# Second copies of k and q by DMA within SBUF, and one block of p's high part on ScalarE

## The chip, the core and the metric

One core of one Trainium2 chip runs the whole program in a single launch. The metric is the device time of the launch in microseconds. Five engines work beside each other, each through its own list of instructions in order: PE (TensorE, matrix products), DVE (VectorE), ACT (ScalarE), POOL (GpSimd) and SP (SyncE, which here issues DMAs). They wait for each other by semaphores.

## The reference

Causal attention with a decay for 4 batches of 8 heads (sequence 576, head size 64), then two MLPs over the 2304 tokens, all in float32:

```python
scores = scale * np.matmul(q, k.transpose(0, 1, 3, 2))
decay = cum[:, :, :, None] - cum[:, :, None, :]        # cum: running sum of log f
scores = np.where(causal, -1000000000.0, scores + decay)
attn = np.exp(scores - max) ; attn = attn / (sum + 1e-09)
x = attn @ v
h = x @ w_in ; x = (max(h, 0) + alpha * min(h, 0)) @ w_out
out = ((x @ w_a) * (x @ w_b)) @ w_o
```

## The kernel before

**Stages.** The program runs attention head by head (32 heads, `u` from 0 to 31, two further rounds to drain). The first MLP runs in two parts: a first part (7 of its 16 blocks of columns) is woven into the attention stage and fills PE between the steps of the heads, as soon as the four batches' attention outputs are there one after the other; the rest, and the second MLP, follow by themselves. The attention stage ends at about 350 us of the span.

**One head.** `stack(n)` turns q and k of head n: PE transposes them into a PSUM bank (`tqk`, two halves of 288 columns), and from there they go to SBUF in the form that the products want. From head 10 on (`NATIVE = 10`) a float32 product is made of parts. k's high part goes to `u1` in partitions 64 to 127 (ACT, line 350) and k's remainder to `u2` (DVE, 353); q's high part goes to `t1` in partitions 0 to 63 (ACT, 352) and its remainder to `t1` in partitions 64 to 127 (DVE, 355). Two second copies complete the operands: `u1`'s high part again in partitions 0 to 63 (POOL, called in line 358 and recorded in line 238 by the helper `dup`), and q's high part again in `t2` (ACT, called in line 357, recorded in line 234). `products` then takes two matmuls for each block of scores: `t1` by `u1` over 128 partitions (line 372) and `t2` by `u2` over 68 (line 373; the last four of these partitions carry the decay). Heads 0 to 9 take a shorter way without second copies.

**Softmax and p.** `softmax_in` masks a block on DVE (385) and exponentiates it on ACT (386). `rinv` makes the reciprocals (DVE, 408 and 409). For a head from 10 on, `p_hi` writes the high half-precision part of each of the five blocks of p (ACT in line 438, or POOL in 440) and `p_lo` the remainder (DVE, 520). When the parts of a group of blocks are there, SP issues a DMA that transposes them (527), and `pv` multiplies by v two heads later. Blocks are numbered by their width: block 3 is 128 rows by 512 columns, block 2 is 128 by 384. An engine for each step stands in the table `eng`, over which `eng0` is laid for steps 0 to 9.

**What sets the order.** The lists `even` and `odd` say in which order the steps of a head are written; a scheduler with a model of times then interleaves them into one order for each engine, which the chip follows as it stands. Tiles named with `_0` or `_1` serve even and odd heads in turn. All DMAs are issued by SP. The scheduler gives the DMAs eight semaphores in turn, and a DMA waits until the one before it on its semaphore has landed.

```python
pe.matmul(o, t1[:, q0:q0 + 128], u1[:, a0:a1], start=start, stop=False)
pe.matmul(o, t2[0:68, q0:q0 + 128], u2[0:68, a0:a1], start=False, stop=stop)
```

Of the kernel before, what the change touches and what calls it, by code (L numbers as in the profile page):

```python
# [40 lines left out]
    odd="ri h3 h2 h0 R rr vs h1 M Q l2 T l3 s2 M h4 s3 l1 M M s1 l0 s0 p0 p1 V W po l4 M".split(),  # L41
    split=0,
    lag=2,
    eng={'U': 'pool', 'xl': 'pool', 'h2': 'act', 'h0': 'pool', 'h1': 'pool', 'nq': 'act', 'x': 'dve'},
    psm=3,
    first=10,
    rates=[0, 1, 1, 1, 0.8, 1.15, 1.15, 0.95],
# [2 lines left out]
    pre=1,  # L50
    we=0,
    es=10,
    eng0={'h3': 'pool', 'U': 'pool', 'h1': 'pool', 'e0': 'act', 'e2': 'act', 'e3': 'dve', 'e4': 'dve'},
    even0=['ri', 's3', 'T', 'p0', 'h2', 'h3', 's2', 'vs', 'h1', 's0', 'Q', 'M', 'M', 'M', 'M', 'l1', 'l2', 'h0', 's1', 'l0', 'l3', 'p1', 'V', 'po', 'W', 'M'],
    odd0=['ri', 'h3', 'h2', 'h0', 'R', 'h1', 'rr', 'M', 'Q', 'l2', 'T', 'l3', 'M', 's3', 'h4', 's2', 'l1', 'l0', 'M', 'M', 's1', 's0', 'p0', 'vs', 'p1', 'V', 'W', 'po', 'l4', 'M'],
)
# [3 lines left out]
NATIVE = _P.get("native", 0)  # L60
# [20 lines left out]
def f32(ap):  # L81
    return ap.bitcast(F32)
# [3 lines left out]
def decay_attention_then_two_mlps(ctx, tc, q, k, v, f, w_in, w_out, alpha, w_a, w_b, w_o, out):  # L86
    nc = tc.nc
    pe, dve, act, pool, sp = nc.tensor, nc.vector, nc.scalar, nc.gpsimd, nc.sync

    left, mid, right = ExitStack(), ExitStack(), ExitStack()  # L90
    def lpool(stack, name, bufs, side="left", **kw):
        return stack.enter_context(tc.tile_pool(name=name, bufs=bufs, side=side, reuse_waits="tile", **kw))
# [133 lines left out]
    def eng(key, default):  # L226
        d = _P["eng"]
        if ap_["u"] < _P.get("es", 0):
            d = dict(d, **_P.get("eng0", {}))
        return {"pool": pool, "act": act, "dve": dve}[d.get(key, default)]  # L230

    def dup(e, o, i):
        if e is act:
            act.copy(o, i)
        elif e is dve:
            dve.tensor_copy(o, i)
        else:
            pool.tensor_scalar(o, i, 1.0, 0.0, op0=ALU.mult, op1=ALU.add)
# [82 lines left out]
    def bank(nm):  # L321
        return ps["at"].tile([128, 512], F32, tag="at", name=nm)

    def stack(n):

        src = nat.pop(n)
        j = n % 2
        t1, t2, u1, u2, tu2 = TU[j]
        if n < NATIVE:
            t2, u2, tu2 = TUN[j]  # L330
        if n >= 2:
            sp.dma_start(tu2[64:68, :SP + S], cum_d[j][n // 2])
        for c in range(2):
            a0, a1 = c * HB, (c + 1) * HB
            pt = bank(f"tqk_{n}_{c}")[:, :HB]
            for t in range(TM):
                rows = src[:, c * TM + t].rearrange("p i d -> p (i d)")
                pe.transpose(pt[:, t::TM], rows, ap_["ident"][:TT, :TT])
            qt, kt = pt[0:64], pt[64:128]
            ks = slice(a0, a1)  # L340
            cuts = [(a0, a1, 0)]
            if c == 1 and j == 1:
                cuts = [(a0, ST, 0), (ST, a1, SR)]
            cuts = [(slice(x - a0, y - a0), slice(x + o, y + o)) for x, y, o in cuts]
            if n < NATIVE:
                dup(eng("nk", "act"), u2[0:64, ks], kt)
                for x, o in cuts:
                    dup(eng("nq", "act"), t2[0:64, o], qt[:, x])
                continue
            act.copy(u1[64:128, ks], kt)  # L350
            for x, o in cuts:
                act.copy(t1[0:64, o], qt[:, x])
            dve.tensor_tensor(u2[0:64, ks], kt, f32(u1)[64:128, ks], op=ALU.subtract)
            for x, o in cuts:
                dve.tensor_tensor(t1[64:128, o], qt[:, x], f32(t1)[0:64, o], op=ALU.subtract)
            for x, o in cuts:
                dup(eng("T2", "act"), t2[0:64, o], qt[:, x])
            dup(eng("U", "pool"), u1[0:64, ks], f32(u1)[64:128, ks])

    def s_view(n, i):  # L360
        if i == 4:
# [247 lines left out]
    def attention():  # L609

        cur = lambda u: 0 <= u < NI
        if LAG == 2:
            load_v(0)
        warm_up(_P.get("wu", [0, 0])[0], "a")
        stack(0)
        warm_up(_P.get("wu", [0, 0])[1], "b")
        load_qk(2)
        yield "W", -1
        for u in range(NI + LAG):
            ap_["u"] = u  # L620
            for op in order(u):
# [10 lines left out]
                elif a in "hl":  # L632
                    if cur(u - 1):
                        (p_hi if a == "h" else p_lo)(u - 1, int(i))
                elif op == "R":
                    if cur(u):
                        softmax_rest(scores_rest(u))
                elif op == "rr":
                    if cur(u):
                        rinv(ap_["smr"][:, 0:1], ap_["rir"][:, 0:1])  # L640
                elif a == "s":
                    if cur(u):
                        softmax_in(u, int(i), scores(u, int(i)))
                elif op == "T":
                    if cur(u + 1):
                        stack(u + 1)
                elif op == "Q":
                    if u and cur(u + 2):
                        load_qk(u + 2)
                elif op == "V":  # L650
                    if cur(u + 3 - LAG):
                        load_v(u + 3 - LAG)
                elif op == "vs":
                    if cur(u + 2 - LAG):
                        split_v(u + 2 - LAG)
                elif op in ("p0", "p1"):
                    if cur(u - LAG):
                        pv(u - LAG, int(i))
                elif op == "po":
                    if cur(u - LAG):  # L660
                        pv_out(u - LAG)
# [68 lines left out]
    if True:  # L730
# [192 lines left out]
        for ri, (p, t0, n) in enumerate(runs):  # L923
            f0, f1 = PASSES[p]
            xh, xl = cur
# [168 lines left out]
```

## Time and profile before

| what | value |
|---|---|
| time, median of 3 runs | 1062.86 us (1062.18 to 1063.13) |
| the profiled execution: time | 1065.95 us |
| the profiled execution: span of its instructions | 1064.1 us |
| PE busy over the span | 1022.4 us, 96% |
| DVE, ACT, POOL busy over the span | 713.4, 487.2, 497.3 us |
| mean granted TensorE clock | 0.997 of full speed |

The span runs from the first to the last instruction of the profiled execution; the rest of its time, 1.85 us, lies around it. Busy time says how long an engine had an instruction in hand; idle time before an instruction is put down to the event that came last. A time in the trace counts from the span's start.

### The profile page before, as it was taken

How to read it: one execution, taken by the hardware profiler on the slowest of the kernel's cores; microseconds unless marked ns; L12 is line 12 of the kernel's file. 1: busy time of each engine (PE TensorE's matmuls, PEld its weight loads, DVE VectorE, ACT ScalarE, POOL GpSimd, SP SyncE). 2: the span in 40 equal slices, each digit the busy share in tenths (PEclk: the TensorE clock that was granted, in tenths of full speed). 3: DMA queues.
4: the chain of work that ended last, by engine and by line, in shares of the span. 5: the costliest groups of instructions: out<-in, count | busy, mean ns of one | idle time of the engine just before them, and what ended most of it. 6: DMA issues, size and time to landing. Idle time of an engine off the chain costs nothing.

```text
span 1064.1 us, 18614 instructions
## 1 busy us (share of the span) xinstructions
PE 1022.4 (96%) x6447; PEld 958.6 (90%) x6447; DVE 713.4 (67%) x1518; ACT 487.2 (46%) x1200; POOL 497.3 (47%) x566
## 2 busy tenths in 40 slices
PE   4999989999999999999999998999999999999998
PEld 3777989989989999999999998899989999899997
DVE  6667988888888456444456558755986658964553
ACT  5777867778777554333343443322432113321110
POOL 4344567567676355333446766522443224531111
PEclk9999999999999999999999999999999999999999
DMA  5545577876877766656667996726328383453623
GB/s 113 135 121 165 141 138 138 202 146 133 180 164 122 210 222 199 224 191 199 186 230 258 340 365 249 304 94 237 103 94 317 113 310 111 137 206 139 247 89 109
DMA packets 221698, 196.27 MB, mean 184 GB/s; under 512 B 138980, under 2 KB 195812, under 8 KB 221604
## 3 DMA queue, kind: packets, MB, share of 16 engines
q1 hardware_dynamic: 221604, 195.08, 61.2%
q8 instruction: 51, 0.84, 0.3%
q14 instruction: 43, 0.35, 0.1%
HBM read 126.83 MB, written 50.17 MB: 166 GB/s over the span
## 4 chain that ended last, share of the span: by engine, by line
PE 52%; DVE 8%; DMA 3%; issue 3%; POOL 2%; ACT 1%; ACTq 0%; DVEq 0%; POOLq 0%; SPq 0%
PE p L674 7%; PE p L676 7%; PE p L675 7%; PE o L676 4%; PE o L674 4%; PE o L675 4%; PE ya L674 3%; PE ya L675 3%; PE ya L676 3%; PE hb L674 3%; PE hb L676 3%; PE hb L675 3%; DMA wr_in<-in_moe_w_in 2%; DMA yq_d<-yhl 1%; POOL yhl L881 1%
## 5 line engine op out<-in xcount | busy, mean ns | idle before, releaser
L674 PE MATMUL p<-yq,w_h 128*128 128x384 f32 x360 | 121.8, 338 | 2.2 <-DVE lu L1043 1.3
L676 PE MATMUL p<-yq,w_h 128*128 128x384 f32 x360 | 121.3, 337 | 0.0
L675 PE MATMUL p<-yq,w_h 128*128 128x384 f32 x360 | 121.2, 337 | 0.0
L1025 POOL TENSOR_TENSOR gg<-tc,gg 128x384 fp32r<-128x384 f32 x36 | 36.7, 1019 | 114.0 <-ACT gg L1024 96.8
L674 PE MATMUL o<-w_o,gg 128*128 128x512 f32 x216 | 84.7, 393 | 1.7 <-ACT gg L1024 1.7
L675 PE MATMUL o<-w_o,gg 128*128 128x512 f32 x216 | 84.8, 393 | 0.0
L671 POOL TENSOR_TENSOR gb<-lt,gb 128x384 fp32r<-128x384 f32 x54 | 55.5, 1028 | 60.4 <-ACT gb L670 60.3
L676 PE MATMUL o<-w_o,gg 128*128 128x512 f32 x216 | 83.2, 393 | 0.0
L1025 POOL TENSOR_TENSOR gg<-td,gg 128x384 fp32r<-128x384 f32 x36 | 38.1, 1059 | 89.5 <-ACT gg L1024 83.7
L386 ACT ACTIVATE s<-s,nm 128x512 f32<-128x512 f32 (+3 forms) x128 | 71.4, 559 | 10.1 <-DVE nm L385 9.3
L1024 ACT CAST gg<-tc 128x384 fp32r<-128x384 f32 x36 | 18.5, 514 | 124.7 <-DVE tc L1023 124.7
L674 PEld LDWEIGHTS p<-yq,w_h 128*128 128x128 f32 x360 | 67.6, 188 | 6.9 <-DVE lu L1043 1.7
L669 DVE SCALAR_TENSOR_TENSOR lt<-lu,nal,hb 128x384 f32<-128x384 f32 x54 | 33.0, 611 | 59.8 <-ACT lu L668 59.8
L675 PE MATMUL ya<-gb,w_out 128*128 128x384 f32 x216 | 72.7, 337 | 0.0
L676 PE MATMUL ya<-gb,w_out 128*128 128x384 f32 x216 | 72.5, 336 | 0.0
L674 PE MATMUL ya<-gb,w_out 128*128 128x384 f32 x216 | 71.0, 336 | 1.2 <-DVE yl L866 1.2
L675 PEld LDWEIGHTS p<-yq,w_h 128*128 128x128 f32 x360 | 67.6, 188 | 3.7
L674 PE MATMUL h<-xh,w_in 128*128 128x288 f32 x224 | 67.5, 305 | 1.0 <-DVE lt L669 1.0
L676 PEld LDWEIGHTS p<-yq,w_h 128*128 128x128 f32 x360 | 67.5, 188 | 0.2
L675 PE MATMUL h<-xl,w_in 128*128 128x288 f32 x224 | 66.5, 298 | 1.2 <-POOL xl L582 1.2
L675 PE MATMUL y<-g,w_out 128*128 128x288 f32 x224 | 67.2, 302 | 0.5 <-POOL g L671 0.5
L385 DVE CUSTOM_DVE_ANT_0 s<-sc,maskz 128x512 f32<-128x512 f32 (+3 forms) x128 | 59.3, 486 | 12.4 <-PE sc L369 11.1
(207 smaller groups left out, 3313.4 us busy)
## 6 DMA issues: line engine op xcount, KB each, us to landing
yq<-yq_d SPq DMA_DIRECT2D x49, 768.0 KB
yq_d<-yhl SPq DMA_DIRECT2D x42, 384.0 KB
yl<-ya_d SPq DMA_DIRECT2D x48, 192.0 KB
po_d<-os SPq DMA_DIRECT2D x36, 256.0 KB
os<-po_d SPq DMA_DIRECT2D x36, 256.0 KB
wr_in<-in_moe_w_in SPq DMA_DIRECT2D x16, 512.0 KB
wr_out<-in_moe_w_out SPq DMA_DIRECT2D x16, 512.0 KB
wr_a<-in_moe_w_a SPq DMA_DIRECT2D x12, 512.0 KB
```

The lines of the kernel that those rows point to most:

```text
L385: dve.tensor_tensor_reduce(s, o, m, -0.125, 3.0e38, ALU.add, ALU.min, nm)
L386: act.activation(s, s, AF.Exp, bias=nm, scale=-1.0, accum_out=sm)
L669: dve.scalar_tensor_tensor(t, u, nal[:, fi:fi + 1], hp[:, :n], op0=ALU.mult, op1=ALU.add)
L671: pool.tensor_tensor(gl, t, f32(gh), op=ALU.subtract)
L674: pe.matmul(o, lh, rh, start=start, stop=False)
L675: pe.matmul(o, lh, rl, start=False, stop=False)
L676: pe.matmul(o, ll, rh, start=False, stop=stop)
L881: pool.tensor_tensor(yh[:, 1], x, f32(yh[:, 0]), op=ALU.subtract)
L1024: ap_["last"] = act.copy(g[:, 0], o).ins
L1025: pool.tensor_tensor(g[:, 1], o, f32(g[:, 0]), op=ALU.subtract)
```

## The change

From head 10 on, the two second copies are no longer made by ACT and POOL. After both halves of the head are in `u1` and `t1`, ACT issues two DMAs from SBUF to SBUF: partitions 64 to 127 of `u1` to partitions 0 to 63 (64 rows of 576 floats), and partitions 0 to 63 of `t1` to `t2` (64 rows of 640 floats). And from step 10 on, `p_hi` of block 3 is made by ACT in line 438, where POOL made it in line 440.

```diff
-    eng={'U': 'pool', 'xl': 'pool', 'h2': 'act', 'h0': 'pool', 'h1': 'pool', 'nq': 'act', 'x': 'dve'},
+    eng={'xl': 'pool', 'h2': 'act', 'h3': 'act', 'h0': 'pool', 'h1': 'pool', 'nq': 'act', 'x': 'dve'},
...
-    eng0={'h3': 'pool', 'U': 'pool', 'h1': 'pool', 'e0': 'act', 'e2': 'act', 'e3': 'dve', 'e4': 'dve'},
+    eng0={'h3': 'pool', 'h1': 'pool', 'e0': 'act', 'e2': 'act', 'e3': 'dve', 'e4': 'dve'},
...
             for x, o in cuts:
                 dve.tensor_tensor(t1[64:128, o], qt[:, x], f32(t1)[0:64, o], op=ALU.subtract)
-            for x, o in cuts:
-                dup(eng("T2", "act"), t2[0:64, o], qt[:, x])
-            dup(eng("U", "pool"), u1[0:64, ks], f32(u1)[64:128, ks])
+        if n >= NATIVE:
+            act.dma_start(f32(u1)[0:64], f32(u1)[64:128])
+            act.dma_start(f32(t2)[0:64], f32(t1)[0:64])
```

The scheduler makes a new order for all engines from head 10 to the end of the first MLP's woven part; behind it the order of every engine is as before. Three places show it. In the rows, `U1`, `T1` and `TU2` are the tiles of `u1`, `t1` and of `t2` with `u2`; `tqk_12_1` is the second half of head 12.

ACT at head 12, before:

```order
L350 CAST U1_0_147<-tqk_12_0_1383 64x288
L352 CAST T1_0_146<-tqk_12_0_1383 64x288
L350 CAST U1_0_147<-tqk_12_1_1393 64x288
L131 ACTIVATE wx_out5_1139<-wr_out5_1137 128x512
L352 CAST T1_0_146<-tqk_12_1_1393 64x288
L504 ACTIVATE xh_1_1472<-pvw_4_0_1293 128x256
L670 CAST g_0_0_1202<-lt_4_1425 128x288
L438 ACTIVATE p16_10_hi_1339<-s_0_151,ri_0_154 128x3x128
L405 ACTIVATE sr_164,smr_167<-sr_164,nmr_166 128x576
L234 CAST TU2_0_148<-tqk_12_0_1383 64x288
L386 ACTIVATE s_1_160,sm_1_162<-s_1_160,nm_1_161 128x384
L234 CAST TU2_0_148<-tqk_12_1_1393 64x288
```

ACT at the same head with the change:

```order
L350 CAST U1_0_147<-tqk_12_0_1378 64x288
L352 CAST T1_0_146<-tqk_12_0_1378 64x288
L350 CAST U1_0_147<-tqk_12_1_1386 64x288
L352 CAST T1_0_146<-tqk_12_1_1386 64x288
L670 CAST g_0_0_1197<-lt_4_1418 128x288
L438 ACTIVATE p16_10_hi_1334<-s_0_151,ri_0_154 128x4x128
L438 ACTIVATE p16_10_hi_1334<-s_0_151,ri_0_154 128x3x128
L405 ACTIVATE sr_164,smr_167<-sr_164,nmr_166 128x576
L504 ACTIVATE xh_1_1465<-pvw_4_0_1288 128x256
L357 DMA U1_0_147<-U1_0_147 64x576
L358 DMA TU2_0_148<-T1_0_146 64x640
```

The two casts to `TU2` are gone, block 3 of p (`128x4x128`) is there, and the two DMAs stand last, behind five instructions that don't belong to the stack; the preparation of a weight (line 131) now stands ahead of the head's casts.

PE, with the change, at the end of the same stretch, where the scores of head 12 begin:

```order
L372 MATMUL sc_11_0_1458<-U1_1_156,T1_1_155 128x128
L373 MATMUL sc_11_0_1458<-TU2_1_157 128x128
L498 MATMUL pvw_4_1_1291<-PT32_9_r_1147,vs_0_169 128x64 x3
L338 MATMUL tqk_13_0_1504<-ident_90,qkn_13_1371 128x96 x3
L338 MATMUL tqk_13_1_1512<-ident_90,qkn_13_1371 128x96 x3
L372 MATMUL sc_12_2_1529<-U1_0_147,T1_0_146 128x384
```

Before, the twelve matmuls of `h_0_0_6` (lines 674 to 676, 128x288) stood between the third and the fourth of these rows; they now come later.

ACT at head 27, before:

```order
L350 CAST U1_1_156<-tqk_27_0_4003 64x288
L352 CAST T1_1_155<-tqk_27_0_4003 64x288
L350 CAST U1_1_156<-tqk_27_1_4013 64x288
L352 CAST T1_1_155<-tqk_27_1_4013 64x224
L352 CAST T1_1_155<-tqk_27_1_4013 64x64
L234 CAST xh_2_2883<-x32_11_1_3796 128x320
L386 ACTIVATE s_0_151,sm_0_153<-s_0_151,nm_0_152 128x384
L234 CAST TU2_1_157<-tqk_27_0_4003 64x288
```

ACT at head 27 with the change:

```order
L350 CAST U1_1_156<-tqk_27_0_3961 64x288
L352 CAST T1_1_155<-tqk_27_0_3961 64x288
L438 ACTIVATE p16_25_hi_3981<-s_1_160,ri_1_163 128x4x128
L438 ACTIVATE p16_25_hi_3981<-s_1_160,ri_1_163 128x3x128
L350 CAST U1_1_156<-tqk_27_1_3969 64x288
L352 CAST T1_1_155<-tqk_27_1_3969 64x224
L352 CAST T1_1_155<-tqk_27_1_3969 64x64
L386 ACTIVATE s_0_151,sm_0_153<-s_0_151,nm_0_152 128x384
L357 DMA U1_1_156<-U1_1_156 64x576
L358 DMA TU2_1_157<-T1_1_155 64x640
```

Both blocks of p that ACT now makes stand between the casts of the first and of the second half. On PE, between the transposes of head 27 and its first product, 18 matmuls of the MLP stand where 30 stood, and 15 of 64 columns (lines 542 to 544) have moved behind that product.

## Rows read from the trace of the kernel before

**Rows 1.** Page, part 1: busy time of each engine.

```profile
PE 1022.4 (96%) x6447; PEld 958.6 (90%) x6447; DVE 713.4 (67%) x1518; ACT 487.2 (46%) x1200; POOL 497.3 (47%) x566
```

**Rows 2.** Two stretches: PE, PEld, DVE, ACT, POOL busy, clock, DMA share, GB/s.

```profile
100.00:150.00 50.00, 45.33 (x333) 42.43 (x332) 45.31 (x129) 38.31 (x111) 29.70 (x42) 0.97 0.64 156
150.00:350.00 200.00, 193.15 (x1728) 183.20 (x1728) 170.18 (x477) 153.44 (x447) 133.60 (x188) 1.00 0.76 154
```

**Rows 3.** Waits of PE from 100 to 345 us: total, times, longest.

```profile
PE pv L542 <- DVE nm L385: 3.7, 5, 1.6
PE sc L372 <- DVE x L576: 2.5, 5, 1.1
PE h L675 <- POOL xl L582: 1.2, 1, 1.2
```

**Rows 4.** Tile TU: the second copy of q; ns min/median/max.

```profile
L234 ACT CAST TU<-tqk x55: 204/386/400, 102.6 to 333.6; 64x288 fp32r<-64x288 f32 x33, 64x224 fp32r<-64x224 f32 x11, 64x64 fp32r<-64x64 f32 x11
```

**Rows 5.** Tile U: the second copy of k.

```profile
L238 POOL TENSOR_SCALAR U<-U x44: 428/431/878, 100.8 to 332.4; 64x288 fp32r<-64x288 f32 x44
```

**Rows 6.** Tile p_hi: block 3 on POOL.

```profile
L440 POOL TENSOR_SCALAR p_hi<-s,ri x22: 694/695/1007, 120.7 to 348.9; 128x512 f16<-128x512 f32 x22
```

**Rows 7.** Groups by form, 150 to 345 us: busy, mean ns, idle before.

```profile
L386 ACT ACTIVATE s<-s,nm 128x512 f32<-128x512 f32 x18 | 13.0, 722 | 2.3 <-DVE nm L385 1.9
L438 ACT ACTIVATE p_hi<-s,ri 128x384 f16<-128x384 f32 x18 | 11.1, 616 | 3.9 <-POOL g L671 1.9 <-DVE ri L409 0.9 <-DMA PT_hi<-p_hi 0.9
L520 DVE SCALAR_TENSOR_TENSOR p_lo<-s,ri,p_lo 128x128 f16<-128x128 f32 x18 | 10.9, 603 | 1.0 <-POOL p_lo L440 0.8
```

**Rows 8.** Tile p_lo: DVE's remainders of blocks 0 and 1.

```profile
L520 DVE SCALAR_TENSOR_TENSOR p_lo<-s,ri,p_lo x44: 340/563/1081, 124.0 to 352.0; 128x128 f16<-128x128 f32 x22, 128x256 f16<-128x256 f32 x22
```

**Rows 9.** Timeline of SP's queue: start, us, two loads of v.

```profile
243.24 0.50 SPq L311 DMA_DIRECT2D vs<-in_v  x1
...
297.09 0.50 SPq L311 DMA_DIRECT2D vs<-in_v  x1
```

**Rows 10.** Timeline of POOL: the instructions that waited for those loads.

```profile
245.66 0.72 POOL L319 TENSOR_TENSOR vs<-vs 128x320 f32<-128x320 f32 x1 [0.95 <-DMA vs<-in_v]
...
301.07 0.72 POOL L319 TENSOR_TENSOR vs<-vs 128x320 f32<-128x320 f32 x1 [2.05 <-DMA vs<-in_v]
```

**Rows 11.** Timeline of ACT at head 12.

```profile
119.67 0.39 ACT L350 CAST U<-tqk 64x288 fp32r<-64x288 f32 x1
...
121.63 0.42 ACT L670 CAST g<-lt 128x288 fp32r<-128x288 f32 x1
...
122.47 0.77 ACT L405 ACTIVATE sr<-sr,nmr 128x576 f32<-128x576 f32 x1
```

**Rows 12.** Timeline of PE at head 12.

```profile
124.95 0.38 PE L674 MATMUL h<-xh,w_in 128*128 128x288 f32 x1
...
126.62 0.66 PE L338 MATMUL tqk<-ident,qkn 96*128 96x96 f32 x6
127.06 0.42 PE L372 MATMUL sc<-U,T 128*128 128x384 f32 x1
```

**Rows 13.** Timeline of ACT at head 27.

```profile
284.65 0.40 ACT L350 CAST U<-tqk 64x288 fp32r<-64x288 f32 x1
...
286.96 0.62 ACT L386 ACTIVATE s<-s,nm 128x384 f32<-128x384 f32 x1 [0.25 <-DVE nm L385]
```

**Rows 14.** Timeline of PE at head 27.

```profile
282.12 0.66 PE L338 MATMUL tqk<-ident,qkn 96*128 96x96 f32 x6
...
291.50 0.30 PE L372 MATMUL scr<-U,T 128*128 128x288 f32 x1
```

**Rows 15.** Chain of waits at the end of attention: start, us.

```profile
348.88 0.67 POOL p_hi L440
...
351.91 0.81 POOL g L671
352.77 0.40 PE y L675
```

## The prediction

> **What bounds the kernel now.** I read the page's busy times first: PE is busy for 96% of the span [rows 1], so only the gaps in PE's work can be won, and a new wait of PE is lost in full unless a later one shrinks by it. The change reaches from head 10 (about 100 us) to the end of attention (about 350 us), so the second view is the busy time of that stretch. PE lacks 4.7 us from 100 to 150 and 6.9 us from 150 to 350, together 11.5 us [rows 2]: this is all that the change could win. Beside it DVE is busy for 170 of 200 us (85%), ACT for 153 (77%) and POOL for 134 (67%) [rows 2]: no engine is full, but each follows an order fixed beforehand, so one late instruction holds all behind it. The third view is what PE waited for: DVE's masking of scores (3.7 us) and DVE's sum of two output halves (2.5 us), both of which free a PSUM bank, and POOL's `xl` (1.2 us), 7.4 us in all [rows 3]. PE does not now wait for the second copies in any sum worth naming.
>
> **What is removed and added.** ACT loses 55 casts to `t2`: 33 of 0.386 us, 11 of 0.204 and 11 between (about 0.34), some 18.7 us [rows 4]. It gains 22 blocks of 128x512 of p. POOL took 0.695 us for one [rows 6]; on ACT no row shows it. Bounds are ACT's block of 128x384, 0.616 us, and its exponential over 128x512, 0.722 us [rows 7]; I take 0.72, the same width, so 15.8 us. It gains 44 DMA issues; SP spends 0.50 us on one of its loads [rows 9], and I take that, 22 us (between nothing, if the engine works on behind the issue, and 44 if a full queue doubles it). ACT's net is +19 us over 22 heads, 0.9 us a head. A head takes 10.8 us (18 blocks of a kind in 195 us, [rows 7]), so ACT goes from 77% to about 85%. I cost this at nothing by itself: its idle fifth covers it. Without that cover all 19 us would fall on PE. POOL loses 44 copies of 0.43 us and 22 of 0.695 us, 34 us or 1.6 us a head [rows 5, 6]; that is worth only what POOL's lateness costs others. PE's and DVE's own instructions stay the same.
>
> **How late the operands come.** The new wait is PE's, for two DMAs. No row shows a DMA within SBUF. The nearest are short loads of v: issued at 243.24 us, the reader started at 245.66 (2.4 us); issued at 297.09, it started at 301.07 (4.0 us), in both cases released by the DMA [rows 9, 10]. I take the middle, 3.2 us, and keep both ends. The Trainium skill's page "DMA: Bandwidth & Descriptors" (section "Issuing engines are not separate DMA queues") says that DMAs issued by different engines run on the same 16 DMA engines and interleave, so ACT's own queue is no shelter. The trace bears on it with DMA engines 76% busy in this stretch and the two prices above, one of them loaded; by the rule's darker reading every transfer would cost the 4.0 us, which is the first rival below.
>
> At **head 12** ACT's cast of the second half of k starts at 119.67 us [rows 11]. Behind it, in the new order: that cast and the one to `T1` (0.40 each), the `g` cast (0.42), two blocks of p (0.72 and 0.62), the exponential of the rest rows (0.77), one cast (0.4), the first DMA's issue (0.5). The second DMA starts at 123.9 and lands at 126.3 to 127.9 us. The weight's preparation now stands ahead of the casts (some 0.7 us, as a pass over 128x512 takes); if nothing absorbs it, the landing is 127.0 to 128.6. PE began the scores of head 12 at 127.06 [rows 12]; but twelve matmuls have left the way, from 124.95 to 126.62, that is 1.67 us, so it will stand there at 125.4, and at the product that needs `t2` some 0.2 later. So PE waits 0.7 to 3.0 us; I take 1.9.
>
> At **head 27** ACT took the first cast at 284.65 [rows 13], with a block of p ahead of it that now comes behind (0.62), so 284.0 to 284.65. Four casts (some 1.7 with the split half), two blocks of p (1.34), an exponential (0.7) and one issue (0.5) follow: the second DMA starts at 288.3 to 288.9 and lands at 290.7 to 292.9. PE stood at the product at 291.50 [rows 14]. Now 12 wide matmuls are missing ahead of it (0.139 each by head 12's twelve, 1.67 us) and 15 narrow ones (an estimate by columns, 15 x 64/288 x 0.139 = 0.46), so it stands there at 289.4, at `t2` at 289.6. It waits 1.1 to 3.3 us; I take 2.2. The odd heads on either side are of the same kind with shorter chains, and a PE made late by one is less late at the next; I count the group once, and take the other heads' copies as hidden by the MLP's matmuls that stand between transposes and scores; without them each would cost PE its full landing, 2.4 to 4.0 us.
>
> **The sum.** New waits: 1.9 + 2.2 = +4.1 us (1.8 to 6.3). Given back: a PE that is later gives DVE and POOL time, and the 7.4 us of present waits shrink; I take half of the new waits, -2.0 (0 to -4.1). At the end of attention the chain runs through POOL: block 3 of p (0.67 us), then remainders and `g`, and PE's product starts on `g` at 352.77 [rows 15]. With that block on ACT this chain is shorter: -0.5 (0 to -0.67). DVE's remainders: a block of 128x128 takes 0.603 us on the mean but 0.340 at best [rows 7, 8], and DVE and POOL work on p at the same time; 22 such blocks could give DVE back 5.8 us, of which PE sees what its waits for DVE allow. I take -1.0 (0 to -3.7, half of 7.4). Sum: +4.1 - 2.0 - 0.5 - 1.0 = +0.6 us. The profiled execution took 1065.95 us, so it would take 1066.55. The median of the runs is 3.09 us lower, and the same change on it gives 1063.5 us. I call 0.2%, 2.1 us, about what a measurement here can tell from no change.
>
> **Behind the waits.** A DMA issued by ACT waits for the last cast, and for the DMA before it on its semaphore. Behind it on ACT stand the next head's exponentials and the MLP's casts; DVE waits for the exponentials' sums, and PE for the banks that DVE frees. SP's later DMAs can wait on ACT's through the same semaphores; its loads of q and k run two heads ahead, which hides some microseconds.
>
> **The rivals.** *Late operands, nothing won back on DVE.* Every transfer takes the loaded 4.0 us, and ACT at 85% issues late. The waits are 3.0 + 3.3 = 6.3; with -2.0 and -0.5, the time is +3.8, 1066.7 us. For it speaks that ACT's order puts foreign work between the casts and the issue; against it that the other of the two loads took 2.4 us, and that ACT keeps 15% idle. It decides against the kernel from a landing of about 3.7 us on. *Relief.* DVE and POOL hinder each other less, so that PE's waits for both halve (-3.7), the end gains 0.5, and the DMAs land in time: -4.2, 1058.7 us. For it speaks 0.603 against 0.340 us; against it that POOL keeps two thirds of its work, its other blocks of p among it. The Trainium skill's page "SBUF — State Buffer" (section "Who interferes with whom") says that a DVE instruction with two inputs in SBUF and a GpSimd instruction that reads SBUF exclude each other, the later one blocking outright. The spread of DVE's remainders agrees with it. *Hidden anyway.* The scheduler's distance suffices, nothing else changes, and only the end's 0.5 us is won: 1062.4 us. For it speaks that 6.9 us lie between head 27's first cast and its product [rows 13, 14], more than issue and landing need by themselves; against it the foreign work that ACT's order puts between.
>
> **How the numbers follow.** Forecast 0.37, late operands 0.30, relief 0.21, hidden 0.12. Relief, with the lucky edge of the forecast and of hidden (0.04), is faster by over 0.2%: 0.25. Late operands with the unlucky edge of the forecast (0.04) is slower: 0.34. The rest is the same: 0.41. The range runs from relief with about a microsecond more of DVE's time won, 1057.5, to all of 6.3 us lost with nothing given back, 1069.0. The forecast's own range is 1060.5 to 1066.5.
>
> **What would show it.** New waits of PE for a DMA on `U` or `TU` of 0.5 to 3 us near 127 us and 290 us, and few elsewhere, would show the main term right; none would show it wrong. ACT's busy time of the stretch with block 3 near 0.72 us, and DMA issues near 0.5 us, show the cost. DVE's 128x128 remainder well under 0.6 us would show relief. The prediction fails if ACT is held at its issues by semaphores for microseconds, or if the chain of waits at the end of attention moves to ACT.

## The result and the profile after

The changed kernel takes 1078.57 us (median of 4 runs, 1077.31 to 1079.97) against 1062.99 us for the kernel before (4 runs on the same chip, 1062.18 to 1063.31): the ratio is 1.0148, with a 95% interval of 1.0130 to 1.0166. That is 15.7 us slower, outside the predicted range. Below, a measured difference in us is the ratio less one, times 1063; the expectations mostly quote differences of medians (15.6 us for this one, and 17.6 for what is 18.1 us here), and they count runs: their second, third and fifth experiments are block 3 alone, the spare copies, and the spare copies in the order of before. The profiled execution took 1079.97 us, and its span is 1078.2 us.

All of it is lost in the attention stage: the product of line 674 on `xh` from which on both kernels have the same order, the first one of `hb`, starts 14.2 us later (422.34 us for 408.18), and the span ends 14.0 us later. Page of the changed kernel, parts 1 and 3:

```profile
PE 1027.0 (95%) x6447; PEld 961.9 (89%) x6447; DVE 714.0 (66%) x1518; ACT 485.4 (45%) x1168; POOL 455.5 (42%) x499
...
q10 hardware_dynamic: 3520, 6.85, 2.9%
```

POOL is relieved by 42 us, and the kernel gains nothing by it [rows 1]. The queue q10 is new: ScalarE's 44 transfers, 6.85 MB. The two stretches of [rows 2], with the same columns:

```profile
100.00:150.00 50.00, 43.87 (x318) 40.47 (x317) 42.24 (x120) 34.13 (x94) 19.37 (x26) 0.97 0.75 172
150.00:350.00 200.00, 187.12 (x1636) 177.84 (x1635) 156.60 (x447) 145.79 (x403) 94.03 (x128) 0.98 0.83 172
```

PE lacks 19.0 us in them, where 11.5 were lacking. DVE, ACT and POOL are all less busy, so none of them became the bound by its work. What rose is the DMA engines' share, from 0.64 and 0.76 to 0.75 and 0.83. Who waited for what, 100 to 345 us for PE and 100 to 365 us for ACT and POOL (total, times, longest):

```profile
PE scr L372 <- ACT lu L668: 3.0, 1, 3.0
...
PE sc L372 <- ACT w_out L139: 2.3, 1, 2.3
...
PE sc L373 <- DMA TU<-T: 0.5, 1, 0.5
...
ACT s L386 <- DVE nm L385: 17.7, 19, 1.9
ACT p_hi L438 <- DMA PT_hi<-p_hi: 11.9, 12, 2.4
...
POOL vs L319 <- DMA vs<-in_v: 22.2, 13, 4.3
...
POOL p_lo L440 <- DMA PT_lo<-p_lo: 16.7, 8, 5.4
```

PE's waits have become small and many [rows 3]. Among the waits for DMAs, those that grew most stand one step behind: ACT and POOL, which write p, now wait 28.6 us for the DMAs that transpose the p of the head before out of the same tile (`p16_hi` and `p16_lo` have one buffer each). In the kernel before the same two lines read:

```profile
ACT p_hi L438 <- DMA PT_hi<-p_hi: 2.5, 2, 1.6
POOL p_lo L440 <- DMA PT_lo<-p_lo: 2.5, 2, 1.4
```

That these waits grew does not yet say that the added transfers made them; experiment 4 comes back to it. At the end of attention they stand in the chain of waits. It ran through POOL [rows 15]; now it runs through the transposing DMAs and ACT (start, us):

```profile
351.67 4.71 DMA PT_hi<-p_hi
356.48 0.73 ACT p_hi L438
...
360.35 5.50 DMA PT_hi<-p_hi
365.96 0.73 ACT p_hi L438
...
369.78 3.30 DMA PT_lo<-p_lo
...
373.21 0.27 PE pv L542
```

Of the 21.5 us from 351.67 to 373.21, 13.5 are transposing DMAs.

**The two places of the prediction.** Head 12 in the timelines of PE, DVE, and ScalarE with its queue (start, us):

```profile
125.25 0.67 PE L338 MATMUL tqk<-ident,qkn 96*128 96x96 f32 x6
128.22 0.41 PE L372 MATMUL sc<-U,T 128*128 128x384 f32 x1 [2.30 <-ACT w_out L139]
...
128.03 0.08 DVE L385 DVE_READ_ACCUMULATOR2_ANT nm<- 128x1 f32 x1
...
121.90 0.47 ACTq L357 DMA_DIRECT2D U<-U  x1
122.12 0.43 ACT L670 CAST g<-lt 128x288 fp32r<-128x288 f32 x1
122.45 0.72 ACT L438 ACTIVATE p_hi<-s,ri 128x512 f16<-128x512 f32 x1
122.47 0.55 ACTq L358 DMA_DIRECT2D TU<-T  x1
```

PE stands at the scores of head 12 and waits 2.3 us, about as predicted (1.9), but not for the copies. By the semaphore events of the trace (a landing here is always the last update of a transfer's semaphore before its next use) U landed 2.55 us after its issue, at 124.45, and T at 125.09. The row names ACT's `w_out` (127.54 to 128.16), which is no operand. The matmul waits for DVE as well, and DVE's reading of the scores before, which frees a PSUM bank, ends at 128.11; DVE works without a gap from 122.8 on, and `w_out` itself had waited 1.6 us for DVE. The program has this product wait for that reading, and of ACT only for the cast to `T1`, done at 122.21. So DVE was late, and the size was right by chance.

The rows show something else that the prediction had otherwise. In ACT's order the two DMAs stand behind `g`, both blocks of p, an exponential and one more cast, and the prediction let them wait for these. They were issued at 121.90 and 122.47, as soon as the casts that they need were done, while ACT still worked on what stands ahead of them. From 100 to 350 us the 44 issues take 25.7 us, and ACT is busy during 19.4 of these.

At head 27 the mechanism is the predicted one. Timelines of PE and of ScalarE's and SP's queues, then a window (columns as in [rows 2]):

```profile
297.13 0.82 PE L372 MATMUL scr<-U,T 128*128 128x288 f32 x2 [3.03 <-ACT lu L668]
...
292.11 0.47 ACTq L357 DMA_DIRECT2D U<-U  x1
...
291.71 0.59 SPq L591 DMA_DIRECT2D xh_d<-xh  x1
292.40 0.58 SPq L591 DMA_DIRECT2D xl_d<-xl  x1
293.03 6.52 SPq L527 DMA_TRANSPOSE PT_r<-p_r  x1
```
```profile
297.00:303.00 6.00, 5.87 (x24) 5.90 (x25) 1.68 (x4) 1.60 (x5) 2.10 (x4) 0.50 1.03 312
```

U's copy is issued between two stores of 1152 KB each, lands after 4.89 us at 297.00, and PE starts at 297.13. The row names ACT's `lu`, but of ACT this product needs only the cast to `T1`, done at 292.55, and of DVE the remainder in `T1`, done at 294.41. It waited 3.0 us (predicted 2.2), and the stall has a second price: from 297 to 303 us the granted clock is 0.50, the lower level of 1.2 GHz.

### The profile page after: what moved, and what is told of

Same layout as the page of the kernel before. It is cut to its first block, busy times and chain, and to the rows that moved or that the text cites. A ratio compares the mean times of both kernels' runs of the same rounds, so it can differ in the third digit from the quotient of the medians.

```text
span 1078.2 us, 18511 instructions
## 1 busy us (share of the span) xinstructions
PE 1027.0 (95%) x6447; PEld 961.9 (89%) x6447; DVE 714.0 (66%) x1518; ACT 485.4 (45%) x1168; POOL 455.5 (42%) x499
## 3 DMA queue, kind: packets, MB, share of 16 engines
q10 hardware_dynamic: 3520, 6.85, 2.9%
## 4 chain that ended last, share of the span: by engine, by line
PE 52%; DVE 8%; DMA 4%; issue 3%; POOL 1%; ACT 1%; SPq 0%; DVEq 0%; ACTq 0%; POOLq 0%
PE p L674 7%; PE p L676 7%; PE p L675 7%; PE o L676 4%; PE o L674 4%; PE o L675 4%; PE ya L674 3%; PE hb L674 3%; PE ya L675 3%; PE hb L676 3%; PE hb L675 3%; PE ya L676 3%; DMA wr_in<-in_moe_w_in 1%; DMA PT_hi<-p_hi 1%; POOL yhl L881 1%
## 5 line engine op out<-in xcount | busy, mean ns | idle before, releaser
L674 PE MATMUL h<-xh,w_in 128*128 128x288 f32 x224 | 68.3, 310 | 3.7 <-DVE lt L669 2.6
L671 POOL TENSOR_TENSOR g<-lt,g 128x288 fp32r<-128x288 f32 x56 | 49.5, 890 | 49.7 <-ACT g L670 44.4
L676 PE MATMUL h<-xh,w_in 128*128 128x288 f32 x224 | 67.7, 303 | 0.0
```

The lines of the kernel that those rows point to most:

```text
L671: pool.tensor_tensor(gl, t, f32(gh), op=ALU.subtract)
L674: pe.matmul(o, lh, rh, start=start, stop=False)
L676: pe.matmul(o, ll, rh, start=False, stop=stop)
```

## The experiments

Three theories stood at the start. **A** (the prediction's): the operands land late and PE waits for them. **B**: the added bytes delay other transfers and what waits for those. **C**: ScalarE is overloaded or held, above all at block 3 of p. From experiment 4 on a fourth: **O**, the order that the scheduler works out anew for every engine costs the time.

**1. The parts apart.** First the DMAs alone (the changed kernel with block 3 of p back on POOL):

```diff
-    eng={'xl': 'pool', 'h2': 'act', 'h3': 'act', 'h0': 'pool', 'h1': 'pool', 'nq': 'act', 'x': 'dve'},
+    eng={'xl': 'pool', 'h2': 'act', 'h0': 'pool', 'h1': 'pool', 'nq': 'act', 'x': 'dve'},
```

> The two copies are DMAs issued by ScalarE, block 3 of p stays on GpSimd. Theory A (the operands land late and PE waits for them) and theory B (the added traffic delays all other DMAs and what waits for these) both expect nearly the whole loss, +11 to +16 us against the kernel before. Theory C (ScalarE is overloaded, above all by block 3 of p, which now also waits in its list for the transposing DMA to free its tile) expects less than half of it, +2 to +7 us.

Measured: 1.0171 [1.0147, 1.0195], +18.2 us. The DMAs alone cost all of the loss and more, above the +16 at which the range of A and B ended. Then block 3 alone, in the kernel before:

```diff
-    eng={'U': 'pool', 'xl': 'pool', 'h2': 'act', 'h0': 'pool', 'h1': 'pool', 'nq': 'act', 'x': 'dve'},
+    eng={'U': 'pool', 'xl': 'pool', 'h2': 'act', 'h3': 'act', 'h0': 'pool', 'h1': 'pool', 'nq': 'act', 'x': 'dve'},
```

> The copies stay on ScalarE and GpSimd, block 3 of p alone moves to ScalarE. Theories A and B expect no loss, -2 to +2 us. Theory C expects +6 to +12 us.

Measured: 1.0077 [1.0053, 1.0101], +8.2 us. So C has something too, and the parts don't add up: 18.2 and 8.2 make 15.7.

**2. Copies that nobody reads.** The kernel before, with the same two DMAs beside its own copies, into spare tiles:

```diff
+        ap_["xu"] = a.tile([128, S], F32, name="xu")
+        ap_["xt"] = a.tile([128, SP], F32, name="xt")
...
+        if n >= NATIVE:
+            act.dma_start(ap_["xu"][0:64], f32(u1)[64:128])
+            act.dma_start(ap_["xt"][0:64], f32(t1)[0:64])
```

> The kernel before, which makes its copies on the engines as it did, and beside it ScalarE issues the same two DMAs for each head into two spare tiles that nobody reads: the traffic and the issues without anyone waiting for the data. Theory A (PE waits for late operands) expects -1 to +3 us. Theory B (traffic delays other DMAs) expects +7 to +15 us, with the loads of q, k and v landing later than in the kernel before. Theory C expects +3 to +6 us for the 44 issues on a ScalarE that has also kept its casts.

Measured: 1.0133 [1.0105, 1.0162], +14.1 us. With no reader no operand can be late, so a loss of this size does not need A. In the changed kernel A has a share all the same, the 3.0 us at head 27.

**3. Another engine issues them.** `act.dma_start` becomes `sp.dma_start` in the changed kernel.

> The changed kernel with the two DMAs issued by SyncE in its list. Theories A and B expect +12 to +20 us: the landings stay late, and SyncE's list, which is already dense, adds its own delay. Theory C (ScalarE held by its issues) expects a gain against the changed kernel, +5 to +10 us over the kernel before.

Measured: 1.0142 [1.0125, 1.0160], +15.1 us. ScalarE's time for the issues and its being held at them isn't it either.

**4. The order held fixed.** A DMA in the program makes the scheduler work out another order on all engines, so theory O had to be told from B. In the next four kernels each instruction gets an issue-only edge to the one that precedes it on its engine in a chosen order (no wait on the chip). With its own order as the chosen one the kernel before is reproduced instruction for instruction on every engine. `rank` is the order, `seq` an engine's instructions:

```diff
+        for a, b in zip(rank, rank[1:]):
+            tc.add_manual_dep(
+                seq[b], seq[a].name,
+                mybir.DependencyInfo(mybir.DependencyClass.NoSync, mybir.DependencyReason.DATA),
+                reason="pin",
+            )
```

The spare copies of experiment 2 in the order of the kernel before:

> The kernel before with the two spare DMAs per head of the third experiment (into tiles that nothing reads), but with the instructions of every engine held to the order that they have in the kernel before; only the DMAs are placed freely on ScalarE. Theory B (the 7 MB of added transfers delay other DMAs and what waits for them): +9 to +15 us, as the same copies cost with their own order. Theory O (the transfers cost little; the loss comes from the other order that the scheduler worked out for all engines once the DMAs were in the program): -1 to +3 us. Theory C (ScalarE held by block 3 of p): 0 to +2 us.

Measured: 1.0170 [1.0141, 1.0199], +18.1 us, above B's range and far from that of O.

The kernel before, without copies, in the order of experiment 2:

> The kernel before, without any added DMA, with the instructions of every engine held to the order that they have in the third experiment (spare copies). Theory B: -1 to +3 us, since nothing is moved. Theory O: +9 to +15 us, since the order alone makes the loss. Theory C: 0 to +2 us.

Measured: 1.0027 [1.0010, 1.0044], +2.9 us. So the transfers cost time at either order, 18.1 us at that of before and 11.2 at this one (14.1 less 2.9), and this order by itself costs some three (at most 4.7 by its interval).

The changed kernel in the order of the kernel before:

> The changed kernel with both of its parts, with all instructions that it shares with the kernel before held to the order of before on each engine; only the two DMAs and block 3 of p are placed freely on ScalarE. Theory B: +9 to +15 us. Theory O: -3 to +3 us, within the range of the prediction. Theory C: +6 to +12 us, since ScalarE still makes block 3 and still waits for the transposing DMA that frees its tile.

Measured: 1.0203 [1.0168, 1.0238], +21.6 us. At the old order the changed kernel loses 6 us more than in its own. Late operands do count here: PE's waits named for the second copy of q come to 8.1 us (5 times, 100 to 365 us).

And the kernel before in the order of the changed one:

> The kernel before, with its copies on GpSimd and ScalarE and block 3 of p on GpSimd, but with all instructions that it shares with the changed kernel held to the order of the changed kernel on each engine. Theory B: -1 to +3 us. Theory O: +9 to +15 us. Theory C: 0 to +2 us.

Measured: 1.0129 [1.0102, 1.0157], +13.7 us. By itself this speaks for O; but here the old copies and block 3 stand on POOL and ACT at places found anew in an order that was made for DMAs, so it shows that this order is bad for the old work, not what it costs the new. With the first two runs of this experiment, O falls as the cause of what the spare copies cost.

For the changed kernel in its own order it stays open. This run has the waits at p's tiles too, without any copy by DMA (the numbers of these lines are 1 higher; 100 to 365 us):

```profile
ACT p_hi L439 <- DMA PT_hi<-p_hi: 5.1, 8, 1.2
...
POOL p_hi L441 <- DMA PT_hi<-p_hi: 16.3, 11, 3.3
...
POOL p_lo L441 <- DMA PT_lo<-p_lo: 6.0, 3, 4.4
```

They come to 27.4 us, against 28.6 in the changed kernel. Nor do the changed kernel's transposing DMAs land much later after their issue: the medians from 150 to 350 us are 3.35 us for PT_lo and 4.31 for PT_hi, against 3.08 and 4.34 before and 2.88 and 4.16 in this run. The loads of q, k and v show the added traffic, with 3.31, 2.84 and 2.93 us against 2.49, 2.43 and 2.76 here. What grew far more is the time until the issue: PT_lo's DMA is issued 4.9 us after DVE's last remainder on the median, where it was 2.0 us before and is 4.6 in this run, whose order on SP is the same. How the 15.7 us of the changed kernel divide between the transfers and the order that came with them is therefore not shown. That the transfers cost time is shown at the two orders above.

With equal orders the two traces can be laid on each other. Before, then with spare copies (its line numbers are 5 higher), the same instructions of PE, DVE, ACT and SP:

```profile
266.23 1.64 SPq L527 DMA_TRANSPOSE PT_hi<-p_hi  x1
271.77 0.62 ACT L438 ACTIVATE p_hi<-s,ri 128x384 f16<-128x384 f32 x1 [0.18 <-DVE ri L409]
274.14 0.47 DVE L576 SCALAR_TENSOR_TENSOR x<-pv,x 64x320 f32<-64x320 f32 x1
274.67 0.44 PE L372 MATMUL sc<-U,T 128*128 128x384 f32 x1 [0.15 <-DVE x L576]
```
```profile
273.62 3.06 SPq L532 DMA_TRANSPOSE PT_hi<-p_hi  x1
282.73 0.62 ACT L443 ACTIVATE p_hi<-s,ri 128x384 f16<-128x384 f32 x1 [3.71 <-DMA PT_hi<-p_hi]
283.38 1.39 DVE L525 SCALAR_TENSOR_TENSOR p_hi<-s,ri,p_hi 128x384 f16<-128x384 f32 x2 [3.91 <-ACT p_hi L443]
285.18 0.47 DVE L581 SCALAR_TENSOR_TENSOR x<-pv,x 64x320 f32<-64x320 f32 x1
285.71 0.69 PE L377 MATMUL sc<-U,T 128*128 128x384 f32 x1 [3.61 <-DVE x L581]
```

Here the whole path of one delay stands in rows. The two spare DMAs were issued at 273.19 and 273.77, around the transposing one. That one lands 9.0 us after its issue (5.0 before), ACT is held 3.7 us at the tile, DVE's remainders wait for ACT, DVE's sum `x` stands behind them in the order, and it is `x` that frees the bank that PE waits for. SP was 7.4 us late at the first row, PE is 11.0 us late at the last, and its matmul now takes 0.69 us instead of 0.44: the granted clock is 0.50 from 285 to 291 us, too.

**5. The dose.** The spare copies in the order of before, with 4 rows of 32 bytes in each, and with half of the rows (`xu` is shown, `xt` alike):

```diff
-            act.dma_start(ap_["xu"][0:64], f32(u1)[64:128])
+            act.dma_start(ap_["xu"][0:4, 0:8], f32(u1)[64:68, 0:8])
```
```diff
-            act.dma_start(ap_["xu"][0:64], f32(u1)[64:128])
+            act.dma_start(ap_["xu"][0:32], f32(u1)[64:96])
```

> The spare copies in the order of before, as in the fifth experiment (+17.6 us), but each of the two DMAs per head carries 4 rows of 32 bytes in place of 144 and 160 KB. If the bytes delay the other DMAs (theory B): -1 to +3 us. If it is the DMAs' issues on ScalarE, their semaphores or their places in the program that cost: +10 to +18 us.

> The spare copies in the order of before with 32 of the 64 rows, so half of the bytes (full size cost +17.6 us, 4 rows of 32 bytes +1.7 us). Cost in proportion to the bytes: +8 to +11 us. Cost that sets in only when the DMA engines are nearly full: +2 to +6 us. Cost per transfer, whatever its size: +13 us or more.

Measured: 1.0016 [1.0007, 1.0025], +1.7 us, and 1.0063 [1.0043, 1.0083], +6.7 us. The same windows of before, of tiny, half and full copies, in this order (columns as in [rows 2]):

```profile
100.00:365.00 265.00, 252.79 (x2196) 239.08 (x2195) 220.22 (x612) 196.28 (x568) 167.64 (x235) 0.99 0.74 156
```
```profile
100.00:365.00 265.00, 250.44 (x2187) 236.97 (x2186) 220.06 (x609) 194.56 (x565) 165.61 (x234) 1.00 0.75 155
```
```profile
100.00:365.00 265.00, 249.91 (x2170) 236.09 (x2169) 219.49 (x609) 194.54 (x564) 164.91 (x235) 0.99 0.81 165
```
```profile
100.00:365.00 265.00, 241.89 (x2064) 228.44 (x2062) 216.93 (x606) 192.73 (x558) 161.42 (x232) 0.98 0.89 172
```

Landings from the semaphore events of these four traces, 150 to 350 us; the DMA share is that of the windows above:

| copies | DMA share | median landing of PT_lo | of PT_hi | time |
|---|---|---|---|---|
| none | 0.74 | 3.08 us | 4.34 us | 0 |
| 4 rows of 32 B | 0.75 | 3.30 us | 4.55 us | +1.7 us |
| half | 0.81 | 4.07 us | 4.94 us | +6.7 us |
| all | 0.89 | 5.39 us | 5.57 us | +18.1 us |

It is what the DMAs move (bytes and packets fall together here), not the issues or semaphores. The first half costs 5 us more than the tiny copies, the second half 11 (give or take 2 and 4 us): the cost grows faster than the bytes as the share nears 0.9. The expectation for a cost in proportion began at 8, the one for a late onset ended at 6, and the value lies between.

**6. Two tiles in turn for p.** If the single tiles carry the loss, a second buffer should take it back. The spare copies in the order of before, then the changed kernel:

```diff
+    p16={'hi': 2, 'lo': 2},
```

> The spare copies at full size in the order of before, as in the fifth experiment (+17.6 us), but with two tiles in turn for the high block rows of p (3.5 KB a partition more) and two for the low ones (1.5 KB), so that the engines that write p don't wait until the transposing DMA of the head before has landed. Theory B1 (the copies delay the transposing DMAs, these hold ScalarE and GpSimd at p's single tiles, and PE waits for what is behind): 0 to +7 us. Theory B2 (the loads and the transposed operands themselves arrive late at PE, the tiles don't matter): +13 to +18 us.

> The changed kernel with the same two tiles in turn for p's high and low block rows, in an order of its own. Theory B1: +1 to +8 us against before in place of +15.6. Theory B2: +12 to +17 us.

Measured: 1.0120 [1.0103, 1.0137], +12.8 us in place of +18.1; and 1.0075 [1.0049, 1.0100], +8.0 us in place of +15.7. The first misses B1's range and lies just below B2's; the second is at the end of B1's. The controls without DMAs, in the old and in a new order:

> The kernel before, without added DMAs, in its own order, with two tiles in turn for p's high and low block rows. If what two tiles gave back in the run with the spare copies (4.8 us) is the traffic's path (theory B1): -1 to +1 us. If it is a gain that they bring to any kernel: -3 to -5 us.

> The kernel before with two tiles in turn for p's high and low block rows, in an order of its own, as the changed kernel with two tiles had one (+8 us). If the 7.6 us that the changed kernel won by them is the traffic's path: -2 to +1 us. If any kernel wins it: -5 to -8 us, which would beat both kernels.

Measured: 0.9984 [0.9974, 0.9994], -1.7 us, and 1.0017 [1.0003, 1.0031], +1.8 us. In the first pair, all at one order, some 3.6 of the 5.3 us would then be the traffic's path and not a gain that any kernel has; with intervals of 1 to 3 us on each of the three runs that is hardly clear of noise. In the second pair each kernel has an order of its own, so its 7.7 us may be the order's as well. Without the waits at the single tiles 12.8 us of loss remain, so these waits are the smaller part of what the transfers cost. In the run with copies and two tiles ACT and POOL hardly wait for the transposing DMAs any more (1.7 us). Of PE's longest waits there the first is in the run with 4 rows of 32 bytes too (4.9 us), and the next three are for the moved data or one step behind:

```profile
PE pv L548 <- DVE nm L391: 4.0, 5, 1.5
PE pv L548 <- DMA PT_r<-p_r: 3.4, 1, 3.4
PE h L681 <- POOL xl L588: 3.3, 2, 2.7
PE sc L379 <- DMA TU<-cum_d: 2.2, 1, 2.2
```

What carries the remaining 12.8 us, one by one, stays open.

**7. ScalarE's block 3.** Alone in the order of before, and left out of the changed kernel with two tiles (the edits are those of experiments 1, 4 and 6):

> Block 3 of p on ScalarE alone (+9 us in the second experiment, with an order of its own), with the instructions of every engine held to the order of before; only the moved block is placed freely on ScalarE. Theory C (ScalarE is late behind the larger block and its wait): +6 to +11 us. Theory O (the cost was the other order): -1 to +3 us.

> The changed kernel with two tiles in turn for p and block 3 of p left on GpSimd, so the two DMAs alone with two tiles. If ScalarE's block 3 is what remains of the loss of the changed kernel with two tiles (+8 us; theory C): -1 to +3 us. If the bytes are what remains (theory B): +6 to +12 us.

Measured: 1.0099 [1.0084, 1.0114], +10.5 us, and 1.0112 [1.0089, 1.0136], +11.9 us. So the block costs about ten by itself, yet beside the DMAs the kernel with it was 4 us faster (8.0 with it, 11.9 without); there the intervals overlap (5.2 to 10.6 us and 9.5 to 14.5) and each kernel has an order of its own. The first is read at the same place as above, in this run's trace (ACT, DVE, PE):

```profile
271.91 1.23 ACT L440 ACTIVATE p_hi<-s,ri 128x512 f16<-128x512 f32 x2
...
273.17 1.75 DVE L524 SCALAR_TENSOR_TENSOR p_hi<-s,ri,p_hi 128x384 f16<-128x384 f32 x2 [0.91 <-ACT p_hi L440]
...
276.09 0.57 PE L372 MATMUL sc<-U,T 128*128 128x384 f32 x1 [1.86 <-DVE x L580]
```

ACT now makes both blocks of p in a row, where POOL made one of them at the same time. DVE's remainders start that much later, `x` behind them too, and PE's 0.15 us of wait has become 1.86. Whether the block helps beside the DMAs, and why, was not tested apart.

The one version that beats both kernels is the kernel before with two tiles for p and its order kept: 0.9984, 1062.5 us in 10 runs beside 1064.5 in 19.

## Why the prediction was wrong

**What failed** is the step that gave the DMAs a price at PE alone. The sum took one landing for the two new operands and called all else hidden; the DMA engines' share of 76% was used only to judge how late the new copies come. The runs show the reverse direction: the new copies make the old transfers late. At the order of before, copies without any reader cost 18.1 us and all but empty ones 1.7; at the spare copies' own order they cost 11.2. The sum had nothing there and should have had some 11 to 16 us. It also had no term for the new order, and how the two share the changed kernel's 15.7 us stays open; the prediction's sentence on semaphores, that SP's later DMAs could be delayed, looked at the same transfers for a reason that the tiny copies exclude.

**ScalarE's +19 us "at nothing by itself".** Its parts were sized well: block 3 took 0.72 us as assumed, the issues 0.47 and 0.59 (assumed 0.50). But the issues took little of the engine's time, 6.3 of 25.7 us at most, and ACT's busy time fell by 1.8 us. That the idle fifth covers them is wrong for the block: +10.5 us alone, and the rows of experiment 7 show at one place what counts in place of ACT's idle share: DVE and a PSUM bank wait behind p in a fixed order.

**The landing**, 3.2 us (2.4 to 4.0), measured 3.4 for U and 4.3 for T on the median, up to 7.3 and 9.0. **Head 27** was right in mechanism and nearly in size (3.0 for 2.2): U went out 3.2 us after the first cast, where 3.7 was reckoned, and landed after 4.9, beyond the 4.0. **Head 12** had the size (2.3 for 1.9) with another cause: DVE was late, and the second DMA, reckoned to start at 123.9 or later, was issued at 122.47. That other heads hide their landings held: beside head 27's, PE's waits named for U or T come to 0.5 us from 100 to 345 us.

**Given back, relief, the end.** DVE's remainder of 128x128 fell from 0.603 to 0.511 us, so the relief exists; it won nothing, as DVE waits for POOL's and ACT's parts instead. The three waits of [rows 3] did shrink, from 7.4 to 0.9 us, more than was assumed; a dozen others of 0.3 to 3.0 us stand in their place. The end of attention gained no 0.5 us: its chain moved to ACT and the transposing DMAs, which the prediction had named as a sign of failure. **The clock** was in no term: the lower level followed a stall and added to it.

**The rivals.** *Late operands* pointed to the right side with the wrong mechanism (and 3.8 us). The rule of the Trainium skill's page "DMA: Bandwidth & Descriptors" (section "Issuing engines are not separate DMA queues"), that transfers of all engines interleave on the same 16, agrees with the traces: at the order of before PT_lo's median landing went from 3.08 to 5.39 us with the spare copies, and moving the issues to SP left the loss as it was (15.1 us for 15.7). The prediction read it as a price for the new transfers, where it is one for the old.

## What to carry to other kernels

A copy moved from an engine to DMA can be paid for by the other DMAs: before costing it, look at the DMA share of its stage and at who waits for a tile that a DMA has yet to read. At a share of 0.74 and an order held fixed, another 0.15 made the transposes' median landing 1.2 to 2.3 us longer and the kernel 18.1 us; a second buffer for the tiles that they read gave 5.3 us of it back. An idle share of an engine is no cover for work that is put ahead of the instruction others wait for. To tell a transfer's cost from that of a new schedule, keep the order and vary the bytes, and do it at the new order too: a wait that is long there may be as long without the transfers.

## What was not expected of the hardware

A stall of PE costs more than its length when the granted clock falls after it. At head 27 the stall was 3.0 us; in the six us that follow, at 0.50, the products of 128x288 start 0.24 us apart, as these rows show, against 0.13 us in the second pair ahead of the stall, by which I estimate another 2.7 us (6 x (1 - 0.13/0.24)).

```profile
299.19 0.44 PE L675 MATMUL h<-xl,w_in 128*128 128x288 f32 x1
299.43 0.44 PE L676 MATMUL h<-xh,w_in 128*128 128x288 f32 x1
```
```profile
291.20 0.29 PE L676 MATMUL h<-xh,w_in 128*128 128x288 f32 x1
291.33 0.29 PE L675 MATMUL h<-xl,w_in 128*128 128x288 f32 x1
```

After head 12's 2.3 us the clock was 0.57 from 129 to 133 us; after a wait of 1.2 us that ended at 210.10 it stayed at 1.00 (204 to 214 us). A DMA issue on ScalarE went out ahead of work that stands before it in ScalarE's order: at head 12 the first at 121.90 us, when `g`, the first of five such instructions, started at 122.12. And a transposing DMA can hold SP for long at its issue: 6.52 us at 293.03, against 1.38 on the median of the same transfer, while two stores of 1152 KB were under way.
